# A fused attention and feed-forward kernel: two thirds of the first product by a seven-product block scheme, its second operand parts made by adding transfers

## The chip, the cores and the metric

One core of one Trainium2 chip runs the whole program. The metric is the device time of one execution in microseconds (us), as the median of several runs. Rows are from one profiled execution. Its engines: PE (TensorE, the matmuls), ACT (ScalarE), DVE (VectorE), POOL (GpSimd) and SP, which issues the loads. Matmuls write PSUM banks of 512 float32 per partition; all other tiles lie in SBUF.

## The reference, cut to what matters

```
x = causal_attention(q, k, v)                       # B=2, H=12, S=448, D=64 -> x[896, 768]
g = sigmoid(x @ w_gate) * (x @ w_val)               # 768 -> 1536, first product
y = g @ w_out                                       # 1536 -> 768, second product
h = y @ w2_in;  a = h * clip(h + 3, 0, 6) / 6       # 768 -> 2048, third product
out = a @ w2_out                                    # 2048 -> 768, fourth product
```

Weights are float64 in memory, activations float32. The result has to be good to float32.

## The kernel before, in words

A float32 operand is carried as two parts, hi (rounded to 12 bits) and lo = x - hi, and a product is three matmul terms: hi·hi, hi·lo, lo·hi. Weights stream in units of 768 values per partition (768 KB of 64-bit words). `load_unit` has SP load a unit three units before its decoding. Decoding takes seven instructions of 768 columns: `dec_scale` on ACT (L105), shift, clamp, join and sign on DVE (L110, L114, L118, L124), which together give the float32 weight `b`; then the parts, hi on ACT (L131) and lo on DVE (L136).

`halves` (L168) is the matmul loop of the first three products: a unit of 128 output features and 768 inputs takes 6 blocks of inputs x 3 terms x 2 batches = 36 matmuls of 448 columns. The first product has 12 feature tiles f, each a gate unit and a value unit: 24 units, 864 matmuls. The batch-0 half of the first two units is done while attention drains. After a tile's two units ACT takes the sigmoid out of PSUM (L604), DVE multiplies the value in (L605), and `split` writes the two parts of g (ACT L159, DVE L160). Units are decoded three ahead (`LA`). The second product is 12 units of 36 matmuls, the third 16; the fourth (L651) has 672 matmuls of 384 columns.

In each engine the instructions stand in the order of the code; only attention is put in order by a small planner, which the change leaves alone. Tiles that share a buffer wait for its last readers.

Of the kernel before, what the change touches and what calls it, by code (L numbers as in the profile page):

```python
# [8 lines left out]
F32 = mybir.dt.float32  # L9
F32R = mybir.dt.float32r  # L10
# [21 lines left out]
def kernel(  # L32
# [12 lines left out]
    nc = tc.nc  # L45
# [6 lines left out]
    # Query tiles begin where a chunk of D keys does.  # L52
# [11 lines left out]
    UN = 768  # L64
    SCALE = 1.0 / float(D) ** 0.5
# [7 lines left out]
    units = []  # L73
    for f in range(K1):
        for w in (w_gate, w_val):
            units.append((w[:, f * P : (f + 1) * P], P))
# [9 lines left out]
    raw_t, part_t, split_t = {}, {}, {}  # L86
# [16 lines left out]
    def dec_scale(u):  # L103
        b = wtmp.tile([P, UN], F32, tag="b", name="b")
        nc.scalar.activation(b, words(u)[0].bitcast(F32), AF.Copy, scale=REBIAS)  # L105
        part_t[u] = b
# [44 lines left out]
    def acc():  # L151
        """The next of four two-bank accumulators, in turn."""
        pool = psum[acc_n[0] // 2 % 2]
        acc_n[0] += 1
        return pool.tile([P, 2, 512], F32, tag="m", name="m")

    def split(hi, lo, src):
        """src (PSUM or SBUF) into its two parts."""
        nc.scalar.copy(hi, src)  # L159
        nc.vector.tensor_sub(lo, src, hi.bitcast(F32))  # L160

    def halves(ps, u, x, k0, first, last, bs=(0, 1), ks=range(6)):
        """ps[f, token] += unit u's [768, 128] block transposed times x, for batches bs."""
        w = split_t[u]
        for i in ks:
            for n, (a, c) in enumerate(TERMS):
                for b in bs:
                    nc.tensor.matmul(  # L168
                        ps[:, b, :S],
                        lhsT=w[a][:, i * P : (i + 1) * P],  # L170
                        rhs=x[c][:, k0 + i, b * S : (b + 1) * S],
                        start=(first and i == 0 and n == 0),
                        stop=(last and i == 5 and n == 2),
                    )

    ps_a = ctx.enter_context(tc.tile_pool(name="ps_a", bufs=2, space=PSUM))
    psum = [ps_a]

    xt = [acts.tile([P, KD, NT], F32R, tag=f"xy{x}", name=f"xt{x}") for x in range(2)]

    with tc.manual_schedule():
        # ================= attention =================
        with ExitStack() as actx:
# [17 lines left out]
            # V by chunks of 64 keys, the first head's over the second's, block diagonal.  # L201
# [168 lines left out]
            def x_out(p, x):  # L370
                b, hp = divmod(p, NPAIR)
                return xt[x][:, hp, b * S : (b + 1) * S]
# [7 lines left out]
            # Chunks that share a PSUM bank, with their columns there: the longest left, and the  # L380
            # longest that still fits.
# [63 lines left out]
            # While the last pairs drain: the first weights, and batch 0's part of their products.  # L445
# [18 lines left out]
            def f_pe(u, i):  # L464
                if i == 0:
                    first_acc.append(acc())
                halves(first_acc[u], u, xt, 0, True, True, (0,), (i,))
# [9 lines left out]
            # Buffers: how many, and (step that takes one, step that gives it back) in turn.  # L477
# [64 lines left out]
            # How far a kind of step falls back, in pairs.  # L542
# [6 lines left out]
            # The tensor engine's clock rises under load: products of zeros keep it busy while the  # L549
            # first pairs start.  # L550
# [18 lines left out]
        # ================= feed-forward =================  # L569
# [4 lines left out]
        def advance(u):  # L574
# [4 lines left out]
        psum.append(  # L579
            ctx.enter_context(  # L580
                tc.tile_pool(name="ps_b", bufs=2, space=PSUM, reuse_waits="tile")
            )
        )
# [4 lines left out]
        u = 0  # L588
        g1 = [gact.tile([P, K2, NT], F32R, tag=f"g{x}", name=f"g1_{x}") for x in range(2)]
        for f in range(K1):  # L590
            pgv = []
            for i in range(2):
                if u < 2:
                    pgv.append(first_acc[u])
                    halves(pgv[i], u, xt, 0, True, True, (1,))
                else:
                    pgv.append(acc())
                    halves(pgv[i], u, xt, 0, True, True)
                if i == 0:
                    advance(u)  # L600
                    u += 1
            pg, pv = pgv
            t = scr.tile([P, NT], F32, tag="t", name="t")
# [6 lines left out]
            u += 1  # L610

        yt = [acts.tile([P, KD, NT], F32R, tag=f"xy{x}", name=f"yt{x}") for x in range(2)]
        for o in range(KD):
            py = acc()
            for s in range(2):
                halves(py, u, g1, 6 * s, s == 0, s == 1)
# [5 lines left out]
        g2 = [gact.tile([P, K2, NT], F32R, tag=f"g{x}", name=f"g2_{x}") for x in range(2)]  # L622
        for f in range(K2):
            ph = acc()
            halves(ph, u, yt, 0, True, True)
# [6 lines left out]
            nc.scalar.mul(g2[0][:, f, :], t, 1.0 / 6.0)  # L632
            nc.vector.scalar_tensor_tensor(
                g2[1][:, f, :], t, 1.0 / 6.0, g2[0][:, f, :].bitcast(F32),
                op0=ALU.mult, op1=ALU.subtract,
            )
            decode_b(u + LA)
# [3 lines left out]
        osb = acts.tile([P, NTT, DM], F32, tag="xy0", name="osb")  # L641
        outs = out.rearrange("(t p) d -> p t d", p=P)
        NS = K2 // 2
        for c in range(2):
# [3 lines left out]
            def block(t, s, w):  # L648
                for i in range(2):
                    for n, (a, e) in enumerate(TERMS):  # L650
                        nc.tensor.matmul(  # L651
                            po[t],
                            lhsT=g2[a][:, 2 * s + i, t * P : (t + 1) * P],
# [14 lines left out]
            # The last two units go by token tile, so that the tiles are done one after another.  # L668
# [44 lines left out]
```

## Time and profile before

| | |
|---|---|
| median of 3 runs | 623.01 us (622.4 to 623.78) |
| span of the profiled execution | 620.4 us |
| busy: PE / DVE / ACT / POOL | 611.8 / 413.4 / 267.0 / 94.3 us |
| granted TensorE clock | 1.000 over the whole span |
| memory traffic | 65.05 MB, mean 105 GB/s |

The profiled execution has no separate time from outside; its span is 2.6 us below the median. In the views a row names engine, line and operation, then output tile <- input tiles, and the mean of one instruction. "Idle before" is how long the engine waited just ahead of such instructions, and for whom.

### The profile page before, as it was taken

The numbers are of one execution on the slowest core, as the hardware profiler recorded it, in microseconds if no ns is written. First come the engines' busy times: TensorE is split into PE (matmuls) and PEld (weight loads), VectorE is DVE, ScalarE is ACT, GpSimd is POOL, SyncE is SP. The second block draws the span as 40 slices with busy tenths as digits, with TensorE's granted clock in tenths as the row PEclk, the third lists the DMA queues.
The fourth block names the chain that finished last, engine by engine and source line by source line (L and its number), as shares of the span: only waits on it lengthen the run. The fifth ranks groups of instructions, "written<-read, shape, count | busy, mean of one in ns | idle before, by whom it ended". The sixth has DMA issues, their size and how long they took to land.

```text
span 620.4 us, 8945 instructions
## 1 busy us (share of the span) xinstructions
PE 611.8 (99%) x3498; PEld 560.2 (90%) x3498; DVE 413.4 (67%) x604; ACT 267.0 (43%) x532; POOL 94.3 (15%) x152
## 2 busy tenths in 40 slices
PE   8999999999999999999999999999999999999997
PEld 4788788999999999999999999999999999999997
DVE  6699997556666666666655666788778888617701
ACT  3898998533333333333233222444454443223200
POOL 4889998300000000000000000000000000000000
PEclk9999999999999999999999999999999999999999
DMA  7664350013333333333333333333333345416102
GB/s 167 139 172 124 76 167 3 1 51 102 107 124 125 103 102 107 123 120 109 103 102 101 102 101 102 102 101 110 119 125 108 101 107 169 135 48 196 46 1 89
DMA packets 80489, 65.05 MB, mean 105 GB/s; under 512 B 34624, under 2 KB 76352, under 8 KB 80448
## 3 DMA queue, kind: packets, MB, share of 16 engines
q1 hardware_dynamic: 80448, 64.50, 35.0%
q8 instruction: 27, 0.44, 0.3%
q14 instruction: 14, 0.11, 0.1%
HBM read 61.73 MB, written 2.75 MB: 104 GB/s over the span
## 4 chain that ended last, share of the span: by engine, by line
PE 94%; POOL 2%; DVE 1%; ACT 1%; issue 1%; DMA 0%; SPq 0%; POOLq 0%; DVEq 0%
PE m L168 61%; PE m L651 19%; PE pav L362 5%; PE s L279 3%; PE pt L335 3%; PE s L289 1%; PE tr L247 1%; POOL pr L322 1%; DVE vpad L562 1%; POOL vpad L241 1%; ACT pr L307 0%; DMA q<-in_q_dram 0%; POOL vpad L234 0%; DVE kl L263 0%; DVE ql L263 0%
## 5 line engine op out<-in xcount | busy, mean ns | idle before, releaser
L168 PE MATMUL m<-xt,hi 128*128 128x448 f32 x576 | 142.5, 366 | 0.0
L131 ACT CAST hi<-b 128x768 fp32r<-128x768 f32 x68 | 56.9, 836 | 185.0 <-DVE b L124 162.9
L168 PEld LDWEIGHTS m<-xt,hi 128*128 128x128 f32 x576 | 107.8, 188 | 8.4
L651 PE MATMUL m<-hi,g 128*128 128x384 f32 x448 | 113.8, 334 | 0.0
L168 PE MATMUL m<-yt,hi 128*128 128x448 f32 x384 | 93.4, 365 | 0.0
L136 DVE TENSOR_TENSOR lo<-b,hi 128x768 fp32r<-128x768 f32 x68 | 64.9, 954 | 40.8 <-ACT hi L131 40.8
L168 PE MATMUL m<-xt,lo 128*128 128x448 f32 x288 | 83.8, 365 | 0.0
L651 PEld LDWEIGHTS m<-hi,g 128*128 128x128 f32 x448 | 80.8, 188 | 0.0
L168 PEld LDWEIGHTS m<-yt,hi 128*128 128x128 f32 x384 | 72.1, 188 | 5.7
L651 PE MATMUL m<-lo,g 128*128 128x384 f32 x224 | 74.8, 334 | 0.0
L168 PE MATMUL m<-g,hi 128*128 128x448 f32 x288 | 70.1, 365 | 0.0
L124 DVE SCALAR_TENSOR_TENSOR b<-raw,b 128x768 int32<-128x768 int32 x68 | 65.9, 968 | 2.3
L118 DVE SCALAR_TENSOR_TENSOR b<-b,raw 128x768 int32<-128x768 int32 x68 | 65.4, 961 | 2.3
L105 ACT ACTIVATE b<-raw 128x768 f32<-128x768 f32 x68 | 61.3, 902 | 0.0
L168 PEld LDWEIGHTS m<-xt,lo 128*128 128x128 f32 x288 | 54.1, 188 | 4.3
L168 PEld LDWEIGHTS m<-g,hi 128*128 128x128 f32 x288 | 54.1, 188 | 4.3
L168 PE MATMUL m<-yt,lo 128*128 128x448 f32 x192 | 54.5, 365 | 0.0
L322 POOL TENSOR_SCALAR pr<-pr,rc 64x64 f32<-64x64 f32 (+3 forms) x96 | 52.3, 562 | 8.7 <-DVE rc L316 7.1
L307 ACT ACTIVATE pr<-s,nm 64x64 f32<-64x64 f32 (+3 forms) x96 | 44.4, 469 | 5.9 <-PE s L289 5.2
L605 DVE TENSOR_TENSOR t<-m,t 128x896 f32<-128x896 f32 x12 | 13.1, 1091 | 47.1 <-PE m L168 47.1
L651 PEld LDWEIGHTS m<-lo,g 128*128 128x128 f32 x224 | 42.0, 188 | 0.0
L362 PE MATMUL pav<-pth,vpad 128*128 128x448 f32 (+6 forms) x168 | 41.0, 309 | 0.0
(64 smaller groups left out, 760.1 us busy)
## 6 DMA issues: line engine op xcount, KB each, us to landing
raw<-in_moe_w_out_dram SPq DMA_DIRECT2D x28, 768.0 KB, 4.4
raw<-in_moe_w_in_dram SPq DMA_DIRECT2D x16, 768.0 KB, 4.6
raw<-in_moe_w_gate_dram SPq DMA_DIRECT2D x12, 768.0 KB, 4.5
raw<-in_moe_w_val_dram SPq DMA_DIRECT2D x12, 768.0 KB, 4.3
k<-in_k_dram SPq DMA_DIRECT2D x24, 112.0 KB, 2.7
q<-in_q_dram SPq DMA_DIRECT2D x24, 112.0 KB, 3.0
v<-in_v_dram SPq DMA_DIRECT2D x24, 112.0 KB, 2.9
out_dram<-osb SPq DMA_DIRECT2D x1, 1344.0 KB, 8.5
```

Of the source, the lines that this page charges most:

```text
L105: nc.scalar.activation(b, words(u)[0].bitcast(F32), AF.Copy, scale=REBIAS)
L118: nc.vector.scalar_tensor_tensor(bi, bi, 3, words(u)[1], op0=ALU.logical_shift_left, op1=ALU.bitwise_or)
L124: nc.vector.scalar_tensor_tensor(bi, words(u)[0], -(2 ** 31), bi, op0=ALU.bitwise_and, op1=ALU.bitwise_or)
L131: nc.scalar.copy(hi, part_t[u])
L136: nc.vector.tensor_sub(lo, part_t.pop(u), split_t[u][0].bitcast(F32))
L168: nc.tensor.matmul(ps[:, b, :S], lhsT=w[a][:, i * P : (i + 1) * P], rhs=x[c][:, k0 + i, b * S : (b + 1) * S], start=(first and i == 0 and ...
L279: nc.tensor.matmul(ps[:, j], lhsT=live["q" + "hl"[a], p][r, Q0[t] : n], rhs=live["k" + "hl"[c], p][r, :n], start=(i == 0), stop=False,)
L307: nc.scalar.activation(pr[:, :, j], ps[:, j].rearrange("p (c d) -> p c d", d=D), AF.Exp, bias=nm[:, j : j + 1], accum_out=sm[:, j : j + 1],)
L322: nc.gpsimd.tensor_scalar(pr[:, :, j], pr[:, :, j], rc[:, j : j + 1], 1.0, op0=ALU.mult, op1=ALU.mult)
L335: nc.tensor.transpose(ps[:, o : o + rows], live["pr", p, t][:, c].rearrange("p j d -> p (j d)"), identf[:rows, r : r + rows],)
L362: nc.tensor.matmul(live["pav", p][:, c * D :], lhsT=vpad[p % NV][a][:, c], rhs=pt[e][:, off : off + S - c * D], start=(c == 0 and m == 0), ...
L651: nc.tensor.matmul(po[t], lhsT=g2[a][:, 2 * s + i, t * P : (t + 1) * P], rhs=w[e][:, i * HC : (i + 1) * HC], start=(s == 0 and i == 0 and ...
```

## The change

**The scheme.** Tiles f = 0 to 3 of the first product are done as before (8 "plain" units, j = 0 to 7, of 36 matmuls). Tiles 4 to 11 are taken two at a time, gate and value apart: 8 pairs p = 0 to 7, even ones gates, odd ones values. The weights of a pair are a 2 x 2 block matrix A (two tiles x two halves of the inputs), x is a 2 x 2 block matrix B (two halves of the inputs x two batches). Their product is made from seven block products P1 to P7 and sums of blocks, in place of eight. A block product (`product`) is 3 input blocks x 3 terms = 9 matmuls of 448 columns, so a pair takes 63 matmuls instead of 72.

**Sums of x.** T1 to T4 are made once by eight additions of 1344 columns on POOL (`t_sums`), behind the last attention work there, and split by ACT and DVE after j = 3 and j = 5 (`t_split`).

**Sums of weights.** For each pair DVE makes S1 to S4, four operations of 384 columns (`w_sums`). The operands come in four groups (`w_g1`: A11 A12; `w_g2`: S2 S1; `w_g3`: S3 S4; `w_g4`: A22) of 768 columns, the last of 384. `group` makes hi by an ACT copy, and lo without DVE: ACT writes -src into the float32r tile lo, which rounds it to -hi, and a transfer issued by POOL adds src to what lies there.

**Outputs.** P1, P6, P7 and P4 gather in one PSUM bank one after another. ACT copies the bank out between them (`P1_out`, `P6_out`, `P7_out`), and the next of the four waits for that copy. P5 and P3 gather in a second bank, P2 in a third; DVE adds these to the copies (`P2_add`, `P7_add`, `P3_add`). `P4_out` and `finish` apply the sigmoid (ACT) or the multiplication (DVE) by blocks.

**Order.** Iteration p runs P1(p), P2(p), P4(p-1), P6(p), P3(p-1), P5(p), P7(p); P4(7) and P3(7) follow the last. g stays float32 until iteration 7, where `g1_split` begins. Later products keep their matmuls and order, with tiles in other places.

```diff
+        def group(src, n=UN, ring=None):
...
+            nc.scalar.copy(hi[:, :n], src)
+            nc.scalar.mul(lo[:, :n], src, -1.0)
+            nc.gpsimd.dma_start(out=lo[:, :n], in_=src.bitcast(F32R), accum_op=ALU.add)
+            return hi, lo
...
+        def product(ps, w, off, nm, first):
+            x = form[nm]
+            for i in range(HK):
+                k = off * HK + i
+                for n, (a, c) in enumerate(TERMS):
+                    nc.tensor.matmul(
...
-            nc.scalar.activation(both(t), pg[:, :, :S], AF.Sigmoid)
-            nc.vector.tensor_mul(both(t), pv[:, :, :S], both(t))
-            decode_a(u + LA)
-            split(g1[0][:, f, :], g1[1][:, f, :], t)
-            decode_b(u + LA)
-            load_unit(u + LA + 3)
...
+        for p in range(NPR):
+            end = p == NPR - 1
+            P1(p)
+            P1_out(p)
+            if p:
+                P7_add(p - 1)
+            w_dec()
+            P2(p)
+            w_g1(p + 1)
+            P2_add(p)
+            if p:
+                P4(p - 1)
+                P4_out(p - 1)
+            P6(p)
+            P6_out(p)
+            w_sums(p + 1)
+            if p:
+                P3(p - 1)
+                P3_add(p - 1)
+            if end:
+                g1_split(0)
+                g1_split(1)
+                g1_split(2)
+            w_g4(p + 1)
+            w_g2(p + 1)
+            P5(p)
+            w_parts()
+            if p:
+                finish(p - 1)
+            P7(p)
+            P7_out(p)
+            if end:
+                g1_split(3)
+                g1_split(4)
+            if not end:
+                w_dec()
+                w_g3(p + 1)
+        P7_add(NPR - 1)
+        P4(NPR - 1)
+        P4_out(NPR - 1)
+        P3(NPR - 1)
```

**First place: after attention.** ACT's order in the kernel before: the last copy of x (L375), decoding (L105, L131) and the first sigmoid (L604).

```order
L375 CAST xt_70<-pav 128x448 [waits PE_49]
L105 ACTIVATE b<-raw 128x768 [waits DMAHW3_49]
L131 CAST hi<-b 128x768 [waits DVE_49]
L604 ACT_TABLE_LOAD
L604 ACTIVATE t<-m 128x896 [waits PE_49]
```

The same place in the changed kernel: sigmoid L841, decoding L113 and L139.

```order
L391 CAST x_73<-pav 128x448 [waits PE_49]
L841 ACT_TABLE_LOAD [waits PE_49]
L841 ACTIVATE raw_0_2303<-m 128x896 [waits Pool_49]
L113 ACTIVATE b<-raw 128x768 [waits DMAHW3_49]
L139 CAST hi<-b 128x768 [waits DVE_49]
```

Decoding of unit 3 now stands behind the table load and the sigmoid of unit 0, which wait for that unit's matmuls.

POOL's order in the changed kernel there: the eight sums of x, then the first pair's adding transfers (L658).

```order
L624 TENSOR_TENSOR tsum<-x_71 128x1344
L624 TENSOR_TENSOR tsum<-x_73 128x1344 [waits DVE_49]
L624 TENSOR_TENSOR tsum<-x_72 128x1344
L625 TENSOR_TENSOR tsum<-tsum 128x1344 [waits Pool_49]
L626 TENSOR_TENSOR tsum<-tsum 128x1344 [waits Pool_49]
L627 TENSOR_TENSOR tsum<-tsum 128x1344 [waits Pool_49]
L628 TENSOR_TENSOR tsum<-tsum 128x1344 [waits Pool_49]
L658 DMA lo<-b 128x768 [waits DVE_49,Activation_49]
```

Before, POOL had nothing behind attention; now these sums run beside the decoding, and 32 transfers follow them.

DVE's order in the changed kernel there: unit 3's decoding (L118 to L144), the multiplication of unit 1 (L843), unit 4's decoding.

```order
L394 TENSOR_TENSOR x_73<-pav,x_73 128x448 [waits Activation_49]
L118 TENSOR_SCALAR raw<-raw 128x768 [waits DMAHW3_49]
L122 TENSOR_SCALAR b<-b 128x768 [waits Activation_49]
L126 SCALAR_TENSOR_TENSOR b<-b,raw 128x768 [waits DVE_49]
L132 SCALAR_TENSOR_TENSOR b<-raw,b 128x768 [waits DVE_49]
L144 TENSOR_TENSOR lo<-b,hi 128x768 [waits Activation_49]
L843 TENSOR_TENSOR raw_0_2303<-m,raw_0_2303 128x896 [waits PE_49,Pool_49]
L118 TENSOR_SCALAR raw<-raw 128x768 [waits DMAHW4_49]
```

DVE's order is as before here; each decoding step waits for the one ahead of it.

**Second place: the end of the last pair.** ACT's order in the changed kernel from P6_out(7) (L787) to P7_out(7) (L796); L167 is hi of g1, L139 hi of a second-product unit, L764 the sigmoid of `finish`.

```order
L787 COPY h<-w 128x448 [waits PE_49]
L167 CAST g_3559<-raw_0_2303 128x896 x2
L167 CAST g_3562<-raw_0_2303 128x896 [waits DMASW6_49,DMASW3_49,DMASW7_49,DMASW2_49,Activation_49]
L139 CAST hi<-b 128x768 [waits DVE_49]
L139 CAST hi<-b 128x768 [waits DVE_49,PE_49]
L764 ACTIVATE raw_1_2607<-raw_1_2607 128x448
L764 ACTIVATE raw_1_2607<-raw_1_2607 128x896 [waits DVE_49]
L796 COPY h<-w 128x448 [waits PE_49]
```

Seven instructions stand between two copies that each let a block product start.

DVE's order there: P3_add(6) (L814), lo of g1 tiles 0 to 4 (L168) and of two weight units (L144), then P7_add(7) (L800).

```order
L814 TENSOR_TENSOR raw_1_2607<-w,raw_1_2607 128x448 [waits PE_49]
L168 TENSOR_TENSOR g_3559<-raw_0_2303,g_3559 128x896 [waits Activation_49]
L168 TENSOR_TENSOR g_3562<-raw_0_2303,g_3559 128x896 [waits DMASW7_49,DMASW6_49,Activation_49]
L168 TENSOR_TENSOR g_3562<-raw_0_2303,g_3562 128x896 [waits Activation_49]
L144 TENSOR_TENSOR lo<-b,hi 128x768 [waits Activation_49] x2
L168 TENSOR_TENSOR g_3597<-raw_0_2303,g_3597 128x896 [waits Activation_49]
L168 TENSOR_TENSOR g_3600<-raw_0_2303,g_3597 128x896 [waits Activation_49]
L800 TENSOR_TENSOR h<-w,h 128x448 [waits PE_49]
```

P7_add(7), which P3(7) waits for, stands behind seven operations of 768 or 896 columns.

## Rows read from the trace of the kernel before

**Rows 1.** The page: span; busy time, share and instructions of each engine.
```profile
span 620.4 us, 8945 instructions
PE 611.8 (99%) x3498; PEld 560.2 (90%) x3498; DVE 413.4 (67%) x604; ACT 267.0 (43%) x532; POOL 94.3 (15%) x152
```

**Rows 2.** The chain that ended last, its end: start us, us, what.
```profile
125.05 375.22 PE m L168 x1851
500.27 116.53 PE m L651 x672
```

**Rows 3.** Matmul line L168: count, ns min/median/max, first to last start.
```profile
L168 PE MATMUL m<-xt,hi x576: 358/365/452, 111.9 to 295.2; 128*128 128x448 f32 x192
...
L168 PE MATMUL m<-g,hi x288: 362/365/369, 295.8 to 382.8; 128*128 128x448 f32 x144
...
L168 PE MATMUL m<-yt,hi x384: 362/365/369, 383.4 to 499.5; 128*128 128x448 f32 x192
```

**Rows 4.** Window 179 to 295.5: length, PE, PEld, DVE, ACT, POOL, PEclk, DMA share, GB/s.
```profile
179.00:295.50 116.50, 116.50 (x577) 107.98 (x576) 77.04 (x96) 40.27 (x48) 0.00 (x0) 1.00 0.34 109
```

**Rows 5.** Timeline of DVE back to back: start us, us, instruction.
```profile
282.51 0.55 DVE L110 TENSOR_SCALAR raw<-raw 128x768 int32<-128x768 int32 x1
282.97 0.55 DVE L114 TENSOR_SCALAR b<-b 128x768 f32<-128x768 f32 x1
283.56 0.96 DVE L118 SCALAR_TENSOR_TENSOR b<-b,raw 128x768 int32<-128x768 int32 x1
284.55 0.96 DVE L124 SCALAR_TENSOR_TENSOR b<-raw,b 128x768 int32<-128x768 int32 x1
285.43 1.08 DVE L160 TENSOR_TENSOR g<-t,g 128x896 fp32r<-128x896 f32 x1
286.43 0.95 DVE L136 TENSOR_TENSOR lo<-b,hi 128x768 fp32r<-128x768 f32 x1
```

**Rows 6.** Timeline of ACT back to back.
```profile
290.40 0.83 ACT L131 CAST hi<-b 128x768 fp32r<-128x768 f32 x1 [3.20 <-DVE b L124]
291.14 0.91 ACT L604 ACTIVATE t<-m 128x896 f32<-128x896 f32 x1
291.95 0.88 ACT L105 ACTIVATE b<-raw 128x768 f32<-128x768 f32 x1
```

**Rows 7.** Lines by form: busy, mean ns, idle before.
```profile
L241 POOL TENSOR_TENSOR vpad<-v,vpad 64x448 fp32r<-64x448 f32 x24 | 27.5, 1147 | 1.9
L351 DVE TENSOR_TENSOR ptl<-pt,pth 128x320 fp32r<-128x320 f32 x12 | 5.6, 471 | 0.1
L378 DVE TENSOR_TENSOR xt<-pav,xt 128x448 fp32r<-128x448 f32 x12 | 7.4, 614 | 4.8 <-ACT xt L375 4.8
L375 ACT CAST xt<-pav 128x448 fp32r<-128x448 f32 x12 | 6.3, 528 | 5.4 <-PE pav L362 5.4
```

**Rows 8.** DMA issues: KB each, median us from issue to landing.
```profile
raw<-in_moe_w_gate_dram SPq DMA_DIRECT2D x12, 768.0 KB, 4.5
k<-in_k_dram SPq DMA_DIRECT2D x24, 112.0 KB, 2.7
```

**Rows 9.** Timelines of POOL and DVE in attention, at 64 us and 108 us.
```profile
64.33 2.41 POOL L322 TENSOR_SCALAR pr<-pr,rc 128x448 f32<-128x448 f32 x2
64.42 1.36 DVE L124 SCALAR_TENSOR_TENSOR b<-raw,b 128x768 int32<-128x768 int32 x1
...
108.31 2.62 POOL L322 TENSOR_SCALAR pr<-pr,rc 128x448 f32<-128x448 f32 x6
```

**Rows 10.** POOL's L322 and DVE's L124: ns min/median/max, first and last start.
```profile
L322 POOL TENSOR_SCALAR pr<-pr,rc x96: 308/526/1806, 13.2 to 114.6; 64x64 f32<-64x64 f32 x24, 128x192 f32<-128x192 f32 x24, 128x320 f32<-128x320 f32 x24, 128x448 f32<-128x448 f32 x24
...
L124 DVE SCALAR_TENSOR_TENSOR b<-raw,b x68: 957/958/1358, 47.6 to 585.4; 128x768 int32<-128x768 int32 x68
```

**Rows 11.** Timeline of ACT at the end of the first plain unit.
```profile
130.09 1.28 ACT L604 ACT_TABLE_LOAD   x1
131.86 0.92 ACT L604 ACTIVATE t<-m 128x896 f32<-128x896 f32 x1 [0.48 <-PE m L168]
```

More of the change, by code (lines that the diff above doesn't have):

```diff
@@ L70 @@
     wsp = ctx.enter_context(tc.tile_pool(name="wsp", bufs=4))
[L73 to L76, printed above, removed]
+    NPL = 4
+    order1 = [(f, v) for f in range(NPL) for v in range(2)]
+    for f in range(NPL, K1, 2):
+        order1 += [(f, 0), (f + 1, 0), (f, 1), (f + 1, 1)]
+    order1.insert(2 * NPL - 3, order1.pop(2 * NPL))
+    order1.insert(2 * NPL - 1, order1.pop(2 * NPL + 1))
+    at1 = {fv: u for u, fv in enumerate(order1)}
+    units = [((w_gate, w_val)[v][:, f * P : (f + 1) * P], P) for f, v in order1]
     for o in range(KD):
@@ L577, in advance @@
             load_unit(u + LA + 3)
[L579 to L583, printed above, removed]
+        psum.append(tc.alloc_tile_pool(name="ps_b", bufs=2, space=PSUM, reuse_waits="tile"))
         def both(t):
             return t.rearrange("p (b s) -> p b s", b=2)
[L588 to L603, printed above, removed]
[L604 to L610 removed]
@@ new lines, in ua, with ub, w_dec, w_parts @@
+        def ua(p):
+            return pairs[p][2]
+        def ub(p):
+            return pairs[p][3]
+        stream = [3]
+        behind = []
+        def w_dec():
+            u = stream[0]
+            stream[0] += 1
+            decode_a(u)
+            load_unit(u + 3)
+            if u > pairs[-1][3] or (u < 2 * NPL + 2 and order1[u][0] < NPL):
+                behind.append(u)
+        def w_parts():
+            while behind:
+                decode_b(behind.pop(0))
+        def w_g1(p):
+            if p < NPR:
+                grp[p, 1] = group(part_t[ua(p)], ring=slots)
@@ new lines, in w_g4, with s_of @@
+        def w_g4(p):
+            if p < NPR:
+                grp[p, 4] = group(part_t[ub(p)][:, HU:], HU, ring=slots)
+                part_t.pop(ua(p)), part_t.pop(ub(p))
+        def s_of(p):
+            if p == 0:
+                if not first_s:
+                    first_s.extend(
+                        gact.tile([P, UN], F32, tag=f"e{6 + i}", name="S") for i in range(2)
+                    )
+                return first_s
+            if p == 1:
+                t = raw1[1].rearrange("p f n -> p (f n)")[:, (K1 // 2 - 2) * NT :]
+            else:
+                t = late["S"]
+            return t[:, :UN], t[:, UN : 2 * UN]
@@ new lines, with w_sums @@
+        first_s = []
+        def w_sums(p):
+            if p >= NPR:
+                return
+            a, b = part_t[ua(p)], part_t[ub(p)]
+            a11, a12, a21, a22 = a[:, :HU], a[:, HU:], b[:, :HU], b[:, HU:]
+            s2, s1, s3, s4 = (t[:, i * HU : (i + 1) * HU] for t in s_of(p) for i in range(2))
+            nc.vector.tensor_add(s1, a21, a22)
+            nc.vector.tensor_sub(s2, s1, a11)
+            nc.vector.tensor_sub(s3, a11, a21)
+            nc.vector.tensor_sub(s4, a12, s2)
@@ new lines, in w_g2, with w_g3 @@
+        def w_g2(p):
+            if p < NPR:
+                grp[p, 2] = group(s_of(p)[0])
+        def w_g3(p):
+            if p < NPR:
+                grp[p, 3] = group(s_of(p)[1])
+        def product(ps, w, off, nm, first):
[4 more added lines that the diff above has]
+                    nc.tensor.matmul(
+                        ps,
+                        lhsT=w[a][:, k * P : (k + 1) * P],
+                        rhs=x[:, c, i],
+                        start=(first and i == 0 and n == 0),
+                        stop=(i == HK - 1 and n == 2),
+                        skip_group_check=True,
+                    )
@@ new lines, with blk, hold_of @@
+        late, banks, hold = {}, {}, {}
+        def blk(f, b):
+            return g_raw(f)[:, b * S : (b + 1) * S]
+        def hold_of(p, nm):
+            f, v = pairs[p][:2]
+            if not v:
+                return {"C11": blk(f, 0), "C12": blk(f, 1), "C22": blk(f + 1, 1)}[nm]
+            if nm == "C22":
+                if (p, nm) not in hold:
+                    hold[p, nm] = scr.tile([P, S], F32, tag="h", name="h")
+                return hold[p, nm]
+            if p not in hold:
+                hold[p] = scr.tile([P, 2, S], F32, tag="t", name="h")
+            return hold[p][:, nm == "C12"]
@@ new lines, in finish_c, with P1, P1_out @@
+        def finish_c(v, g, src):
+            if v:
+                nc.vector.tensor_mul(g, src, g)
+            else:
+                nc.scalar.activation(g, src, AF.Sigmoid)
+        def P1(p):
+            banks[p] = [
+                ps_w.tile([P, 512], F32, tag=f"w{(3 * p + i) % 8}", name="w")[:, :S]
+                for i in range(3)
+            ]
+            product(banks[p][0], grp[p, 1], 0, "B11", True)
+        def P1_out(p):
+            nc.scalar.copy(hold_of(p, "C11"), banks[p][0])
@@ new lines, in P2, with P2_add, P6, P6_out @@
+        def P2(p):
+            product(banks[p][2], grp.pop((p, 1)), 1, "B21", True)
+        def P2_add(p):
+            h = hold_of(p, "C11")
+            nc.vector.tensor_add(h, banks[p][2], h)
+        def P6(p):
+            product(banks[p][0], grp[p, 2], 0, "T2", False)
+        def P6_out(p):
+            nc.scalar.copy(hold_of(p, "C12"), banks[p][0])
+        def P5(p):
+            product(banks[p][1], grp.pop((p, 2)), 1, "T1", True)
+        def P7(p):
+            product(banks[p][0], grp[p, 3], 0, "T3", False)
@@ new lines, in P7_out, with P7_add, P4, P4_out @@
+        def P7_out(p):
+            nc.scalar.copy(hold_of(p, "C22"), banks[p][0])
+        def P7_add(p):
+            h = hold_of(p, "C22")
+            nc.vector.tensor_add(h, banks[p][1], h)
+        def P4(p):
+            product(banks[p][0], grp.pop((p, 4)), 0, "T4", False)
+        def P4_out(p):
+            f, v = pairs[p][:2]
+            finish_c(v, blk(f + 1, 0), banks[p][0])
+        def P3(p):
+            product(banks[p][1], grp.pop((p, 3)), 1, "B22", False)
+        def P3_add(p):
+            h = hold_of(p, "C12")
+            nc.vector.tensor_add(h, banks[p][1], h)
@@ new lines, in finish, with plain_unit @@
+        def finish(p):
+            f, v = pairs[p][:2]
+            finish_c(v, blk(f + 1, 1), hold_of(p, "C22"))
+            finish_c(v, g_raw(f), hold[p].rearrange("p b s -> p (b s)") if v else g_raw(f))
+        for i in range(2):
+            early[at1[NPL + i, 0]] = gact.tile([P, UN], F32, tag=f"e{4 + i}", name="b")
+        plain = {}
+        def plain_unit(j):
+            f, v = divmod(j, 2)
+            if j < 2:
+                ps = first_acc[j]
+                halves(ps, at1[f, v], x_of, 0, True, True, (1,))
+            else:
+                ps = acc()
+                halves(ps, at1[f, v], x_of, 0, True, True)
+            plain[v] = ps
@@ new lines, in plain_out @@
+        def plain_out(j):
+            f, v = divmod(j, 2)
+            t = g_raw(f)
+            if v == 0:
+                nc.scalar.activation(both(t), plain[0][:, :, :S], AF.Sigmoid)
+            else:
+                nc.vector.tensor_mul(both(t), plain[1][:, :, :S], both(t))
+        NJ = 2 * NPL
+        for j in range(NJ):
+            plain_unit(j)
+            if j == 0:
+                tt = t_sums()
+            plain_out(j)
+            if j < NJ - 3:
+                w_dec()
+                w_parts()
+            if j == 3:
+                t_split("T3")
+                t_split("T1")
+            if j == 5:
+                t_split("T2")
+                t_split("T4")
+                raw1.append(gact.tile([P, K1 // 2, NT], F32, tag="xy1", name="raw1_1"))
+            if j == NJ - 7:
+                w_dec()
+            elif j == NJ - 6:
+                w_dec()
+                w_g1(0)
+                w_sums(0)
+                w_g4(0)
+            elif j == NJ - 3:
+                w_g2(0)
+                w_dec()
+            elif j == NJ - 2:
+                w_g3(0)
@@ new lines, with home @@
+        late["S"] = acts.tile([P, 4 * HU], F32, tag="r01", name="S")
+        for pool in reversed(psum):
+            pool.release()
+        ps_w = tc.alloc_tile_pool(name="ps_w", bufs=1, space=PSUM, reuse_waits="tile")
+        homes = (
+            (acts, "r00"), (acts, "r01"), (acts, "r10"), (gact, "rT2"), (gact, "rT1"),
+            (gact, "rT3"), (gact, "rT4"), (acts, "r11"),
+        )
+        place = {}
+        def home(i, name):
+            if i // 3 not in place:
+                pool, tag = homes[i // 3]
+                place[i // 3] = pool.tile([P, 3, NT], F32R, tag=tag, name=name)
+            return place[i // 3][:, i % 3]
@@ new lines @@
+        P7_add(NPR - 1)
+        P4(NPR - 1)
+        P4_out(NPR - 1)
+        P3(NPR - 1)
+        g1_split(5)
+        g1_split(6)
+        P3_add(NPR - 1)
+        finish(NPR - 1)
+        for f in range(7, 10):
+            g1_split(f)
+        w_dec()
+        w_parts()
+        for f in range(10, K1):
+            g1_split(f)
+        u = stream[0] - 3
+        ps_w.release()
+        psum[:] = 2 * [
+            ctx.enter_context(tc.tile_pool(name="ps_c", bufs=4, space=PSUM, reuse_waits="tile"))
+        ]
@@ L613, with y_of @@
+        yt = [gact.tile([P, KD, NT], F32R, tag=f"xy{x}", name=f"yt{x}") for x in range(2)]
+        def y_of(c, k, b):
+            return yt[c][:, k, b * S : (b + 1) * S]
         for o in range(KD):
```

91 lines of the change are left out of this document (75 added, 16 removed).

## The prediction

> **What bounds the kernel now.** The page comes first: PE is busy 611.8 of 620.4 us, DVE two thirds, ACT 43% [rows 1]. Then the chain that ended last: from 125 us on it is PE alone, 1851 matmuls of L168 and 672 of L651, with nothing between [rows 2]. The window over plain first-product work agrees: PE busy 116.50 of 116.50 us at full granted clock, DVE 77, ACT 40, POOL nothing, DMA share 0.34 [rows 4]. So a matmul taken out is worth its pitch, and any operand that comes late costs its lateness. Pitch: 432 matmuls of 448 columns lie between the first of the second product (295.8) and the first of the third (383.4), 202.8 ns each [rows 3]; the 365 ns in the row is the length of one, overlapped with the next.
>
> **What it removes.** 8 pairs x 9 matmuls = 72, x 202.8 ns = **14.6 us**. The later products keep theirs.
>
> **Pairs in steady state.** An iteration is 63 matmuls, 12.8 us, a block product 1.8 us. DVE by pitches back to back [rows 5]: shift 0.46, clamp 0.59, join 0.99, sign 0.88, twice: 5.8; three additions out of PSUM of about 0.55 (the 448-column one lasts 0.614, and ends overlap) 1.6; four sums of 384 columns at about 0.5 (0.471 for 320) 2.0 [rows 7]; a value pair's multiplications 2.1. That is 9.4 to 11.5 of 12.8. ACT [rows 6, 7]: hi and -hi, 0.74 and 0.81, for 3.5 groups, two scalings, three copies of 0.45, a gate pair's sigmoids 1.7: 8.5 to 10.3. Both are hidden. If one were not, each microsecond over would cost 8.
>
> **The adding transfers** have no row: no transfer here adds, none goes from SBUF to SBUF, none is issued by POOL. A load of 112 KB lands after 2.7 us, one of 768 KB after 4.5 [rows 8], so plain data of 384 KB would land after about 3.5. Twice the bytes (both operands are read) would give 4.4, and up to 1 us goes to a load that shares the engines. I take **5.4 us**, an estimate nearer the larger row. What it must meet: the group A11 A12 of the next pair is issued some 6 us into an iteration and its lo is wanted 0.4 us into the next, so up to about 7.2 us costs nothing, and each microsecond beyond costs 8. Only before pair 1 is it tighter: pair 0 runs five block products, 9.1 us, and the group is issued at 4.6. That costs **0.7 us** (nothing below 4.7). The Trainium skill ("DMA: Bandwidth & Descriptors", Anatomy of one DMA, SWDGE path) fits a POOL-issued transfer as 2.0 us plus bytes at 436 GB/s; that gives an estimate of 2.9 us here and no wait, 0.7 us less in the sum; no run yet shows it.
> Room on the DMA engines: 0.34 of 116.5 us for 16 loads [rows 4] is 2.5 us of all sixteen per load. An iteration has two loads, 5.0, and 3.5 full transfers at 1.2 (bytes once) to 2.5 (twice): 9.3 to 13.6 of 12.8.
>
> **The sums of x on POOL.** Its nearest row is the same operation on 448 columns, 1.147 us [rows 7]. Tripled that is 3.4; if the shortest POOL operation there, 0.31 [rows 10], were all fixed cost, 2.8. I take **3.2 us**, so 25.6 for eight, from 125.2, where PE's last attention product frees the memory [rows 2]. Alone they would be done by 151, ahead of their splits, and cost nothing. They are not alone: DVE decodes units 3 and 4 then. The trace shows what the two engines do to each other. At 64.33 two operations of POOL's L322 took 2.41 us, while at 108.31 six of them took 2.62; inside the slow stretch DVE's L124 took 1.36 [rows 9] against a median of 0.958. L322 goes from 0.308 to 1.806 [rows 10]. L378 also works beside POOL, but one of its inputs is PSUM, and its mean of 0.614 [rows 7] leaves no room for such waits. I read this as taking turns: an operation with both inputs in SBUF waits until POOL's current one is done (0.40 there, about one L322), and POOL waits while DVE's runs. With sums of 3.2 us a turn is 3.2 us.
> The Trainium skill ("SBUF — State Buffer", Who interferes with whom) says that a DVE instruction with two SBUF inputs and a GpSimd one that reads SBUF exclude each other for the whole instruction. The trace agrees up to 0.4 us of wait, and no row shows a longer one. By the rule the loss worked out next stands; were 0.4 us the most that DVE ever waits, it would vanish in the slack.
>
> **The ledger after attention** (three POOL sums are over before DVE needs the turn). The sigmoid of unit 0 begins only when PE is done with it, 131.9 [rows 11]; in the new order its table load, 1.28, comes after that wait and the scaling of unit 3 after the sigmoid, so the clamp can start at 135.0. It gets in at 135.3. Then sum 4 to 139.0, join, sum 5 to 143.1, sign, hi by 144.9 and sum 6 beside it to 147.2, lo until 148.1. Unit 3 was wanted at 142.5 (21 units of 7.3 us back from 295.8 [rows 3]): its hi is 2.3 late, its lo 2.4 more. Unit 1's multiplication, sum 7 to 151.2, shift and clamp, sum 8 to 155.4, join, sign, hi, lo 159.3: unit 4, wanted at 154.6, loses 3.9. Now POOL is out of the way, but DVE is behind: until unit 8 it has units 5 to 8 (13.7 with their two lo), four sums (2.1), a multiplication (1.0) and two waits for hi (0.9 each): 178. Units 6 and 8 lose 0.5 and 3.6, unit 9 1.1. In all **13.8 us**. With 2.8 us a sum the same ledger gives 10.8, with 3.4 15.8, and without turns 0: then unit 3 is ready at 139.
>
> **The tail of the last pair**, counted from the start of iteration 7. P7(7) ends at 12.8. ACT does P6_out(7) at 7.4, then three hi of g1 (0.85 each, to 10.4), two weight hi (11.9), sigmoids of 448 and 896 (13.2) and only then P7_out(7), to 13.7. P4(7) starts 1.0 late and ends at 15.6. DVE, from 9.7: lo of g1 0 to 2 (1.03 each, 12.8), two weight lo (14.6), lo of g1 3 and 4, whose hi follow P7_out (16.8), then P7_add(7), to 17.4. P3(7) starts 1.8 late. Together **2.9 us**. The remaining g1 parts come at about one a microsecond and are wanted every 1.2 us: just in time.
>
> **The sum**, as a difference (the profiled span, 620.4, lies 2.6 us under the median; I take the difference from the median, 623.0): 623.0 - 14.6 + 13.8 + 0.7 + 2.9 = **625.8 us**.
>
> **The rivals.**
> *Turns hold but short ones* (A, the forecast): 622.8 to 627.8 by the two prices of a sum, 621.5 to 630 with the transfer's between 4.5 and 7.2. For it: the collisions in attention, which fit the remainder of one POOL operation. Against: none there was over 1.4 us.
> *POOL's sums do not hold DVE* (B, the other side): if the turn passes inside a long operation, decoding loses a few tenths a step, unit 3 has some 3 us of slack, and the sum is 623.0 - 14.6 + 0.7 + 2.9 = 612.0. The point from which it decides: the loss has to fall below 11.0 us, which it does when a sum holds DVE under about 2.8 us.
> *Half of it* (D): the turn passes in the middle, some 7 us lost: 619.
> *Transfers bound the pairs* (C): landing after 9 us gives 1.8 x 8 = 14.4 more, 626 without turns and 640 with; the bytes-twice price on the DMA engines 0.9 x 8 = 7 more. For it: adding is unlike any row. Against: 384 KB is half a load, which lands in 4.5. It decides alone from about 8.5 us of landing.
> That the new matmuls are slower than the old has no support: their length is 365 ns in all three products, whatever they read [rows 3].
>
> **How the numbers follow.** A 0.42, B 0.24, C 0.20, D 0.14. 0.2% (1.25 us) is what a measurement of this kernel can tell from no change. Faster by more: B, most of D, a tenth of A: 0.39. Within: a fifth of A and the rims of the others: 0.11. Slower: 0.50. The point is A's. The range, 611.5 to 632, runs from B with quick transfers to A with transfers a microsecond too slow; outside are most of C with A and B's lowest end. A's own range is 621.5 to 630.
>
> **What will show it.** PE's idle time should lie at three places: some 13 us between 142 and 186 us, before L176 matmuls that wait for hi and lo; under 1 us before pair 1; about 3 us before P4(7) and P3(7). POOL's L624 to L628 should last 2.8 to 3.4 us alone and longer beside DVE's L126, L132, L144, and those should last 3 to 4 us in places instead of 0.96. Between iterations PE should have no gap: the first matmul with lo of a group waits for POOL's transfer otherwise, and the DMA table gives its landing, below 7.2. I am wrong if DVE's decoding keeps its 0.96 us beside the sums (B), or if PE waits once in every iteration (C).

## The result and the profile after

The changed kernel takes 627.44 us (623.63 to 628.0 in ten runs) against 622.38 us of the kernel before on the same chip: ratio 1.006, interval 1.0042 to 1.0079. It is slower, by 5.1 us; the forecast was 625.8.

The page of the changed kernel: span, busy times, and two DMA queues, of which the second carries the adding transfers (packets, MB, share of 16 engines).

```profile
span 626.2 us, 8994 instructions
...
PE 607.0 (97%) x3426; PEld 550.5 (88%) x3426; DVE 447.7 (71%) x652; ACT 313.2 (50%) x612; POOL 148.9 (24%) x192
...
q1 hardware_dynamic: 80448, 64.50, 34.6%
q0 software_dynamic: 4608, 11.01, 10.7%
```

PE has 72 matmuls less than in [rows 1] and 4.8 us less busy time, yet the span grew by 5.8. (1.7 of these lie in attention, which neither kernel does differently: from 75 to 80 us the granted clock was 0.66 in this execution and 1.00 in that of the kernel before. Six of the other runs end the same attention where it ended before.) The chain that ended last, PE alone in [rows 2], now passes to DVE and to transfers:

```profile
136.60 3.23 DVE b L122
139.86 3.75 DVE b L126
143.63 3.69 DVE b L132
...
198.10 4.97 DMA lo<-b
...
261.72 8.07 DMA lo<-b
...
292.16 3.09 DVE g L168 x3
295.25 1.74 DVE lo L144 x2
296.99 2.03 DVE g L168 x2
```

What PE waited for, over the span: total, times, longest.

```profile
PE m L176 <- ACT hi L139: 5.9, 2, 3.8
...
PE w L732 <- DMA lo<-b: 1.6, 3, 0.8
PE w L732 <- DVE h L800: 1.4, 1, 1.4
...
PE m L176 <- DVE lo L144: 1.0, 1, 1.0
PE w L732 <- ACT h L796: 0.9, 1, 0.9
```

Three places: the plain units wait for hi and lo (L139, L144), pairs for a transfer, the last pair for the two queued instructions of the tail (L796, L800). The windows of the plain and the pair stage, with the columns of [rows 4]:

```profile
126.50:192.90 66.40, 59.47 (x269) 52.86 (x269) 53.20 (x49) 26.00 (x31) 30.48 (x12) 0.92 0.35 98
192.90:301.50 108.60, 104.54 (x505) 94.16 (x505) 85.79 (x131) 78.78 (x119) 23.77 (x28) 1.00 0.91 209
```

The eight plain units take 66.4 us; without waits they take 54.2, as in the kernel before (below). So 12.2 us are lost ahead of the pairs. The pairs take 108.6; 576 matmuls of the same work take 116.7 in the kernel before, so 504 take 102.1, and 6.5 are lost there. Their DMA share is 0.91, where it was 0.34 [rows 4]. Why the plain units are late, DVE's and POOL's timeline show:

```profile
136.60 3.22 DVE L122 TENSOR_SCALAR b<-b 128x768 f32<-128x768 f32 x1 [6.26 <-ACT b L113]
139.86 3.74 DVE L126 SCALAR_TENSOR_TENSOR b<-b,raw 128x768 int32<-128x768 int32 x1
143.63 3.68 DVE L132 SCALAR_TENSOR_TENSOR b<-raw,b 128x768 int32<-128x768 int32 x1
148.21 2.82 DVE L144 TENSOR_TENSOR lo<-b,hi 128x768 fp32r<-128x768 f32 x1 [0.90 <-ACT hi L139]
150.95 1.08 DVE L843 TENSOR_TENSOR raw<-m,raw 128x896 f32<-128x896 f32 x1
...
154.86 0.96 DVE L126 SCALAR_TENSOR_TENSOR b<-b,raw 128x768 int32<-128x768 int32 x1
...
126.81 12.60 POOL L624 TENSOR_TENSOR tsum<-x 128x1344 f32<-128x1344 f32 x4 [9.90 <-PE pav L378]
139.37 3.42 POOL L625 TENSOR_TENSOR tsum<-tsum 128x1344 f32<-128x1344 f32 x1
142.87 3.63 POOL L626 TENSOR_TENSOR tsum<-tsum 128x1344 f32<-128x1344 f32 x1
146.57 3.65 POOL L627 TENSOR_TENSOR tsum<-tsum 128x1344 f32<-128x1344 f32 x1
150.29 3.65 POOL L628 TENSOR_TENSOR tsum<-tsum 128x1344 f32<-128x1344 f32 x1
```

Unit 3's clamp, join, sign and lo last 2.8 to 3.7 us each, and each ends 0.4 to 0.8 us after a POOL sum does: sum, step, sum, step. The clamp (L122) waits for the sum that ends at 139.4, the join for the one that ends at 142.8. L843, which reads PSUM, keeps its 1.08 us in the middle of this, and at 154.86, with the sums over, a join is 0.96 again.

### The profile page after: what moved, and what is told of

Same layout as the page of the kernel before. It is cut to its first block, busy times and chain, and to the rows that moved or that the text cites. A ratio compares the mean times of both kernels' runs of the same rounds, so it can differ in the third digit from the quotient of the medians.

```text
span 626.2 us, 8994 instructions
## 1 busy us (share of the span) xinstructions
PE 607.0 (97%) x3426; PEld 550.5 (88%) x3426; DVE 447.7 (71%) x652; ACT 313.2 (50%) x612; POOL 148.9 (24%) x192
## 3 DMA queue, kind: packets, MB, share of 16 engines
q0 software_dynamic: 4608, 11.01, 10.7%
## 4 chain that ended last, share of the span: by engine, by line
PE 76%; DVE 10%; DMA 6%; ACT 3%; POOL 2%; issue 2%; SPq 0%; ACTq 0%; DVEq 0%
PE m L176 37%; PE m L1011 19%; PE w L732 6%; DMA lo<-b 5%; PE pav L378 4%; PE s L295 3%; PE pt L351 3%; DVE b L126 2%; DVE b L132 1%; DVE b L122 1%; PE tr L263 1%; PE pt L456 1%; POOL pr L338 1%; PE s L305 1%; DVE raw L118 1%
## 5 line engine op out<-in xcount | busy, mean ns | idle before, releaser
L139 ACT CAST hi<-b 128x768 fp32r<-128x768 f32 x52 | 43.4, 836 | 161.7 <-DVE b L132 139.6
L144 DVE TENSOR_TENSOR lo<-b,hi 128x768 fp32r<-128x768 f32 x52 | 51.4, 991 | 34.8 <-ACT hi L139 34.8
L132 DVE SCALAR_TENSOR_TENSOR b<-raw,b 128x768 int32<-128x768 int32 x68 | 68.6, 1009 | 2.3
L126 DVE SCALAR_TENSOR_TENSOR b<-b,raw 128x768 int32<-128x768 int32 x68 | 68.2, 1002 | 2.3
L113 ACT ACTIVATE b<-raw 128x768 f32<-128x768 f32 x68 | 61.4, 903 | 2.1 <-DMA lo<-b 1.3
L122 DVE TENSOR_SCALAR b<-b 128x768 f32<-128x768 f32 x68 | 40.5, 596 | 26.3 <-ACT b L113 26.2
L176 PE MATMUL m<-x,hi 128*128 128x448 f32 x192 | 52.4, 387 | 5.9 <-ACT hi L139 5.9
L732 PE MATMUL w<-T,hi 128*128 128x448 f32 x192 | 54.9, 367 | 0.9 <-ACT h L796 0.9
L176 PEld LDWEIGHTS m<-x,hi 128*128 128x128 f32 x192 | 37.5, 199 | 10.1 <-ACT hi L139 6.7
L732 PE MATMUL w<-x,hi 128*128 128x448 f32 x144 | 41.2, 367 | 1.4 <-DVE h L800 1.4
L118 DVE TENSOR_SCALAR raw<-raw 128x768 int32<-128x768 int32 x68 | 41.6, 612 | 0.0
```

The lines of the kernel that those rows point to most:

```text
L118: nc.vector.tensor_scalar(lower, lower, 29, None, op0=ALU.logical_shift_right)
L122: nc.vector.tensor_scalar(b, b, UPPER_MAX, -UPPER_MAX, op0=ALU.min, op1=ALU.max)
L126: nc.vector.scalar_tensor_tensor(bi, bi, 3, words(u)[1], op0=ALU.logical_shift_left, op1=ALU.bitwise_or)
L132: nc.vector.scalar_tensor_tensor(bi, words(u)[0], -(2 ** 31), bi, op0=ALU.bitwise_and, op1=ALU.bitwise_or)
L139: nc.scalar.copy(hi, part_t[u])
L144: nc.vector.tensor_sub(lo, part_t.pop(u), split_t[u][0].bitcast(F32))
```

## The experiments

Stages, from the starts of the matmuls in each profiled execution; "pairs" reaches to the first matmul of the second product, "then" from there to the first of the fourth. Medians stand beside that of the kernel before, measured together with each.

```
                       median / before   plain   pairs   then
before                 622.38             54.2   116.7   204.3   (pairs: 16 units)
changed                627.44 / 622.38    66.4   108.6   204.3
e1_no_sums             615.48 / 623.27    54.2   109.7   204.3
e2_short_sums          625.78 / 623.27    64.5   107.9   204.3
e3_no_transfers        621.61 / 623.27    65.4   105.0   204.3
e4_tail                625.71 / 623.27    65.4   106.5   205.8
e5_scale_first         624.92 / 622.89    65.0   108.1   204.3
e7_g1_dve              627.09 / 622.89    66.9   107.6   204.3
e8_dve_sums            623.60 / 622.89    54.2   116.6   204.3
e12_npl6               620.27 / 622.89    83.4    85.9   204.4   (12 units, 6 pairs)
e15_swap               623.67 / 622.41    66.2   107.3   204.3
e13_npl6_swap          619.16 / 622.41    83.4    83.8   204.4   (12 units, 6 pairs)
```

The theory was that POOL's sums and DVE's decoding take turns, an instruction at a time, and that this makes the plain stage late. Its rivals: the later place of unit 3's scaling; DVE having no time in any case; and, for the pairs, that transfers or queues cost more than they show.

**Without the sums** (`t_sums` returns the hi parts of x and issues nothing).

```diff
-            for r, x in ((r11, xb[0][0]), (r12, xb[0][1]), (r22, xb[1][1]), (r21, xb[1][0])):
-                add(r, x[:, 0].bitcast(F32), x[:, 1].bitcast(F32))
...
-            sub(r21, r21, r11)
+            r11, r12, r21, r22 = (xb[h][b][:, 0].bitcast(F32) for h in range(2) for b in range(2))
```

> Leaves out the eight POOL sums of x; T1 to T4 are the hi parts of x. Turns (POOL's long sums hold DVE's decoding): the 12.3 us lost between the first plain unit and the first pair go, DVE's L122, L126, L132 and L144 are all under 1 us, no half clock after 144 us, so 627.4 - 12.3 = about 615. Rival, decoding is late by its new place behind the first sigmoid alone: unit 3 stays late and some 5 us or more of the loss stay, 620 or more.

615.48 us, ratio 0.988 (0.9823 to 0.9936), and the plain stage is 54.2 us without a wait and at a granted clock of 1.00, although unit 3's scaling still stands behind the sigmoid. The whole loss there is due to the sums, and the kernel without them is 7.8 us faster than the kernel before (four runs, 612.8 to 620.1).

**Shorter sums** (24 operations of 448 columns).

```diff
-                add(r, x[:, 0].bitcast(F32), x[:, 1].bitcast(F32))
...
+                for k in range(HK):
+                    add(r[:, k], x[:, 0, k].bitcast(F32), x[:, 1, k].bitcast(F32))
...
```

> The same sums in 24 operations of 448 columns instead of 8 of 1344. Turns of one operation: each of DVE's steps beside them waits at most 1.2 us instead of 3.2, unit 3 is ready about 144 instead of 151, the loss ahead of the pairs falls from 12.3 to 2 to 4 us: 617 to 619. Rival, the two engines share a port by bytes: POOL's 25 us are taken from DVE in any case and the time stays within 2 us of 627.4.

625.78 us; the plain stage lost 10.3 instead of 12.2. The size of a turn follows the size of a sum, as DVE's and POOL's timeline show:

```profile
135.98 1.79 DVE L126 SCALAR_TENSOR_TENSOR b<-b,raw 128x768 int32<-128x768 int32 x1
137.81 1.79 DVE L132 SCALAR_TENSOR_TENSOR b<-raw,b 128x768 int32<-128x768 int32 x1
...
154.60 1.80 DVE L132 SCALAR_TENSOR_TENSOR b<-raw,b 128x768 int32<-128x768 int32 x1
156.32 1.51 DVE L118 TENSOR_SCALAR raw<-raw 128x768 int32<-128x768 int32 x1
...
125.15 15.47 POOL L625 TENSOR_TENSOR tsum<-x 128x448 f32<-128x448 f32 x12 [9.91 <-PE pav L378]
140.58 19.63 POOL L630 TENSOR_TENSOR tsum<-tsum 128x448 f32<-128x448 f32 x12
```

A join or sign beside a sum waits 0.83 us where it waited 2.7. But the sums last until 160 instead of 154, and thirteen steps of units 3 to 6 are lengthened instead of six of units 3 and 4: by 11.0 us in all, where it was 13.8. Units 3 and 4 come in time; unit 6 is 5.6 us late and unit 8 1.9. (Units 5 and 7 are weights of the first pair; the plain ones are 0 to 4, 6, 8 and 9.) My expected 617 to 619 was wrong: each wait is shorter, yet their total falls by a fifth only. The rival (within 2 us) was right on the time, though DVE loses 11 us and not the 25 that POOL works.

**Scaling first.**

```diff
+            if j:
+                plain_out(j)
             if j < NJ - 3:
                 w_dec()
                 w_parts()
+            if not j:
+                plain_out(j)
```

> ACT scales unit 3 ahead of the first sigmoid, as in the kernel before, so its decoding can start 8 us earlier. Turns: the eight sums take as many turns from DVE's steps wherever decoding starts; unit 3 comes in time, unit 4 is then some 7 us late, and the plain stage still takes 65 us or a little less, 626. Rival, the late place of the scaling is the cause of the loss ahead of the pairs: 5 us or more come back, 622 or less.

624.92 us, plain stage 65.0. Unit 3 is in time, unit 4 5.5 us late, since the turns of unit 3 begin at once (L118 2.48, L122 3.45, L126 3.73, L132 3.73 us). The place of the scaling is not the cause.

**The sums on DVE** (steps of 1344 columns between units, units decoded in the order in which they are wanted, scaling first, T1 to T4 split after j = 5 and 6).

```diff
-            add, sub = nc.gpsimd.tensor_add, nc.gpsimd.tensor_sub
+            add, sub = nc.vector.tensor_add, nc.vector.tensor_sub
...
+            if j < 4:
+                steps[2 * j]()
+                steps[2 * j + 1]()
...
```

> The eight sums of x as DVE operations (about 1.6 us each, 12.6 us of DVE) between the decoding of units in the order in which they are wanted; POOL does nothing there; unit 3 is scaled first. POOL beside DVE is what costs (25 us of POOL work take some 25 us of turns): PE then loses 7 us or less up to the second pair instead of 12, 620 to 622, and no DVE step is over 1.7 us. Rival, DVE has no time to spare there at all: the sums cost their 12.6 us on PE too and the time stays at 626 to 628.

623.60 us. DVE's lines in the plain stage (xcount | busy us, mean ns):

```profile
L124 DVE SCALAR_TENSOR_TENSOR b<-b,raw 128x768 int32<-128x768 int32 x7 | 6.7, 959 | 0.2
...
L623 DVE TENSOR_TENSOR tsum<-x 128x1344 f32<-128x1344 f32 x4 | 6.1, 1551 | 0.0
```

A sum takes DVE 1.55 us where POOL takes 3.15 or more, no step waits, and the plain stage loses nothing. What is pushed back is the work for the first pairs: PE waits 2.1 us for P1_out(0), which stands behind splits of T on ACT, and 2.3 for a transfer of the third pair; its granted clock falls behind both (0.97 over the stage), and the pair stage gives back 8 us of the 12. So POOL beside DVE is what costs in the plain stage. The time lies between the two forecasts, and the rival is right in part: DVE and ACT have no room for all of the sums there.

**Six plain tiles** (`NPL = 6`, one sum or split to a unit).

> As the run with DVE sums, but six plain tiles and six pairs, so that sums and splits are spread over twelve units, one or two to a unit. 54 matmuls saved instead of 72: 10.9 us. If DVE's time ahead of the pairs is the only limit, PE has no wait over 0.5 us before the first pair, 3 us are lost at the last pair, 3 to 4 to transfers and 1 at the second product: 618 to 620, faster than both kernels. Rival, pairs are themselves slower than 12.8 us and lose what they save: 622 or more.

620.27 us (five runs), ratio 0.9951 (0.9931 to 0.9971): faster than both kernels, with three pairs of tiles instead of four, and just above the 618 to 620 expected. The plain stage has no wait, and what PE still waits for is in the pairs and at the first matmul of the second product (L174):

```profile
PE w L733 <- DMA lo<-b: 3.9, 3, 1.5
...
PE w L733 <- DVE h L801: 1.4, 1, 1.4
...
PE m L174 <- DVE h L815: 1.0, 1, 1.0
...
PE w L733 <- ACT h L797: 0.8, 1, 0.8
```

378 matmuls take 76.6 us at the pace of the kernel before, and the pairs take 85.9. So 9.3 of the 10.9 us saved are lost again, most of them to transfers and the tail; why six pairs wait longer for transfers than eight (3.9 us against 1.6) is left open.

**Without the transfers** (lo of the pairs' weights stays -hi).

```diff
-            nc.gpsimd.dma_start(out=lo[:, :n], in_=src.bitcast(F32R), accum_op=ALU.add)
```

> Leaves out the 32 adding transfers; lo of the pairs' weights stays at -hi. Transfers cost their four visible waits and no more: 2.9 us less, 624.5; loads of the first product land after 4.5 us again instead of 6.6, DMA share in the pairs falls from 0.88 to about 0.4. Rival, by keeping the DMA engines busy and GpSimd writing descriptors they also delay DVE and the loads: 5 us less or more, under 622.

621.61 us, which is the rival's time, though the pair stage falls by 3.6 only, to 105.0, and its DMA share to 0.37. Its remaining loss, 2.9, is the tail but for 0.3. Against the kernel before, measured with each, the gain is 6.7 us (from 5.1 above to 1.7 below), more than the stage shows. The plain stage differs by 1.0 and attention by 1.7 between the two profiled executions, but neither shows a part of the transfers: e4_tail, which keeps them, has the same plain stage of 65.4 and the same attention, and both differences are stretches of half clock (see the end). What else the medians differ by is left open. With the transfers, the landing times were (KB each, median us):

```profile
raw<-in_moe_w_gate_dram SPq DMA_DIRECT2D x12, 768.0 KB, 6.8
...
lo<-S POOLq DMA_DIRECT2D x14, 384.0 KB, 5.1
lo<-b POOLq DMA_DIRECT2D x8, 384.0 KB, 7.0
```

**The group A11 A12 by DVE** (lo by a subtraction, 8 transfers less).

```diff
+            if by_dve:
+                nc.vector.tensor_sub(lo[:, :n], src, hi[:, :n].bitcast(F32))
+                return hi, lo
```

> lo of the group A11 A12 is made by a DVE subtraction instead of a transfer, in every pair (8 of 32 transfers less, 1 us more of DVE per iteration). If the landing of this group is what PE waits for between pairs, those waits (2.7 us in all) go, loads of the first product land under 6 us, and the time is about 625. Rival, DVE has no room for it (12.4 of 12.8 us in a value pair): the sums of weights come later, PE waits for the other groups instead, 627 or more.

627.09 us. PE no longer waits for a transfer, but 1.3 us for P1_out; the pair stage is 1.0 us shorter and the plain stage 0.5 longer, as the first subtraction (0.95 us of DVE) stands ahead of unit 8's decoding. The cost mostly moved. The time is the rival's, but not by its way: PE waits for no other group.

**Transfers issued earlier** (-hi and the transfer ahead of the hi copy), in the changed kernel and in the one with six plain tiles.

```diff
+            nc.scalar.mul(lo[:, :n], src, -1.0)
+            nc.gpsimd.dma_start(out=lo[:, :n], in_=src.bitcast(F32R), accum_op=ALU.add)
             nc.scalar.copy(hi[:, :n], src)
-            nc.scalar.mul(lo[:, :n], src, -1.0)
-            nc.gpsimd.dma_start(out=lo[:, :n], in_=src.bitcast(F32R), accum_op=ALU.add)
```

> The changed kernel with one thing moved: in each group -hi and the transfer come ahead of the hi copy, so the transfers are issued 0.75 us earlier. If landing is what PE waits for at the start of pairs (2.7 us in four or five waits), most waits fall by 0.75 us each: the pair stage 106 instead of 108.6 us, the time 625. Rival, the DMA engines are full (share 0.88 in the pairs) and earlier issue only queues earlier: the waits stay within 0.2 us.

> The same move in the kernel with six plain tiles and sums on DVE, whose waits for transfers were 1.0 to 1.7 us at three places: they fall to 0.3 to 1.0, and the time from 620.3 to 618 to 619. Rival, as above: within 0.5 us of 620.3.

623.67 and 619.16 us. The pair stages fall by 1.3, half of what was expected, and by 2.1. In the changed kernel PE then waits for a transfer once, 1.1 us, where it waited three times, 1.6 in all; with six plain tiles it waits 1.3 us for groups of b and 0.8 for one of sums, where it waited 3.9. The 3.8 us between the medians 627.44 and 623.67 are more than the stage shows, and the rest is left open: the profiled execution was the longest of its ten (627.21). 619.16 has the ratio 0.9957 (0.9933 to 0.9982); it is not told apart from the one without the move.

**The tail** (the sigmoids of finish(6) behind P7_out(7), g1 tiles 3 and 4 behind P7_add(7)).

```diff
-            if p:
+            if p and not end:
                 finish(p - 1)
             P7(p)
             P7_out(p)
             if end:
-                g1_split(3)
-                g1_split(4)
+                finish(p - 1)
...
         P7_add(NPR - 1)
+        g1_split(3)
+        g1_split(4)
```

> In the last iteration the two sigmoids of finish(6) stand behind P7_out(7) on ACT, and g1 tiles 3 and 4 are split behind P7_add(7). If the queues in front of these two are the cause of the waits before P4(7) and P3(7) (2.6 us), both fall under 0.3 us and the time is 624.8. Rival, the lateness only moves to the second product, whose g1 parts come later: PE waits there for g1 and the time stays within 1 us of 627.4.

625.71 us, between the two forecasts. The pairs are 2.1 shorter, the second product 1.5 longer; PE now waits 0.6 us for P7_out and twice 0.5 for g1:

```profile
PE w L732 <- ACT h L796: 0.6, 1, 0.6
...
PE m L176 <- DVE g L168: 0.5, 1, 0.5
PE m L176 <- ACT g L167: 0.5, 1, 0.5
```

The queues are what held P4(7) and P3(7), but the work in them is wanted just as soon: nearly all of the tail only moves.

## Why the prediction was right, step by step

- **72 matmuls less, 14.6 us.** Right: 504 matmuls in the pairs, and without transfers (e3) the pair stage is their 102.1 us and 2.9 more, nearly all of it the tail.
- **Turns, 13.8 us.** Right in mechanism, measured 12.2. The first four sums took 3.15 us each (12.60 in all) against the 3.2 taken, DVE's steps 2.8 to 3.7 us against the 3 to 4 foretold. The condition was too narrow as stated: not only operations with two inputs were held, but also the clamp and the shift, which read one tile (3.22 and 2.40 us instead of 0.55). The ledger's single waits were off, and that its sum came near is in part luck. The clamp had to wait for the fourth sum, not the third, so that unit 3's hi was 3.8 late and its lo 1.0; unit 4, which was to cost 3.9, was not waited for, unit 8 was, 2.1. That is 6.9 us of idle PE; the other 5.3 are the same matmuls at a slower pace (59.5 us busy instead of 54.2), most of it at half clock, which the ledger did not have. DVE's lateness alone makes some 11.2 of the 12.2 (see the end). (L322's 0.308 and 1.806 were of two shapes; 64x64 alone goes from 0.31 to 1.80, so that reading holds.) A wait for POOL's whole instruction, in attention never over 0.4 us, reaches 2.8 us here. The Trainium skill ("SBUF — State Buffer", Who interferes with whom) has a DVE instruction with two SBUF inputs and a POOL one that reads SBUF exclude each other for the whole instruction; the trace agrees now at this length too.
- **Transfers, 0.7 us.** Too small: 3.6 us by e3. Where I expected a gap before pair 1 alone, four of seven iterations begin 0.3 to 1.0 us late by the starts of their matmuls, 2.4 in all (the view of waits counts three, by idle time), and the matmuls behind these waits follow each other after 0.207 us or more instead of 0.203, which makes most of the rest. The landing, taken as 5.4, is 5.1 for the sums' groups and 7.0 for A11 A12, at the edge of the 7.2 worked out as free, and the second queue's 10.7% of 626.2 us for 28 full transfers is 2.4 us of all 16 engines each: the price of twice the bytes, the upper of my two bounds. So the pairs run at a DMA share of 0.91. The Trainium skill's fit ("DMA: Bandwidth & Descriptors", Anatomy of one DMA, SWDGE path), which gave 2.9 us, does not hold for these adding transfers beside loads.
- **Tail, 2.9 us.** Right: in e3 P4(7) is 1.0 late and P3(7) 1.6, where 1.0 and 1.8 were foretold.
- **Sum.** -14.6 + 12.2 + 3.6 + 2.9 = +4.1, which is what the two profiled spans differ by without the 1.7 in attention; between the medians it is 5.1, and the forecast was +2.8. Turns came out 1.6 lower than forecast and transfers 2.9 higher: that the errors go against each other is luck. (A slip in A's own range: with a landing of 4.5 its terms give 622.1, not 621.5.)

Rival B, the sums hidden, gave 612.0; with the sums gone e1 takes 615.5, and the 2.9 by which transfers cost more than forecast make most of that difference. C, PE waiting once in every iteration, was not reached.

## What to carry to other kernels

An engine that sits idle is not free if its work holds up another: before moving work to POOL, look in the trace for DVE operations with all inputs in SBUF that lengthen beside it (here from 0.96 to 3.7 us), and charge each such step up to the whole length of a POOL instruction. Cutting the instructions shorter spread the loss and removed little of it (10.3 us instead of 12.2); giving the work to DVE, in half the time and spread over more units, took it out of the plain stage. And a scheme that saves matmuls at the bound engine has to be paid in places with slack: with six plain tiles it saves 54 instead of 72 and is the faster one.

## What was not expected of the hardware

A wait of PE can cost more than its length. During the wait that ends at 148.2 us, and again after the one that ends at 176.3, the granted clock falls, and the matmuls run at half clock for some microseconds; the window of the plain stage has a granted clock of 0.92. PE's timeline of the changed kernel, two or four matmuls a line:

```profile
152.00 1.70 PE L176 MATMUL m<-x,hi 128*128 128x448 f32 x4
...
179.91 1.62 PE L176 MATMUL m<-x,hi 128*128 128x448 f32 x4
181.37 0.57 PE L176 MATMUL m<-x,lo 128*128 128x448 f32 x2
181.78 0.99 PE L176 MATMUL m<-x,hi 128*128 128x448 f32 x4
```

Sixteen matmuls start 0.373 us apart instead of 0.207, 2.7 us in all, at 1.2 instead of 2.4 GHz. The first stretch costs nothing of its own, since unit 8 would have been late anyway: in e4_tail it is longer (granted clock 0.53 from 145 to 156 us), the wait for unit 8 shrinks from 2.1 to 0.7 us, and the plain stage takes 65.4 us. The second adds some 1.0 us: in e3_no_transfers and e4_tail the clock stays 1.00 from 174 to 183 us, where it is 0.76 here from 176 to 183, and both plain stages take 65.4 instead of 66.4. A wait need not bring such a stretch: e3's at this place is as long, 2.2 us. In the pairs of the changed kernel, with waits up to 1.4 us, the granted clock is 1.00; in those of e8_dve_sums it falls behind the waits of 2.1 and 2.3 us, to 0.72 from 186 to 192 and 0.66 from 211 to 216.
